# Moving the last unit's k^T v ahead of its scores, into a PSUM bank of an earlier unit

## Chip, cores, metric

The kernel runs on one core of one Trainium2 chip. The metric is device time in microseconds (us) of that core, the median over several executions; lower is better. All timed runs told here are in the fast state, at a granted TensorE clock of 0.999 to 1.000.

## The reference

Causal retention over 8 batches x 8 heads x 576 positions x 64, then a mixture of four experts, all computed for every token. Cut to what matters:

```python
def _attn_ref(q, k, v):                      # (8, 8, 576, 64) each
    scores = scale * q @ k.transpose(0, 1, 3, 2)
    Dmat = where(rel >= 0, gamma ** rel, 0)  # per-head decay, causal
    return (scores * Dmat) @ v

def _moe_ref(x, domain_probs, w1, w2):       # x: (4608, 512)
    p = domain_probs / (domain_probs.sum(-1, keepdims=True) + 1e-9)
    for e in range(4):                       # w1: (4, 512, 1024), w2: (4, 1024, 512)
        out += p[:, e:e+1] * (relu(x @ w1[e]) @ w2[e])
```

## The kernel before

The kernel folds the decay into q and k, so that attention becomes chunks: scores inside a chunk with a 0/1 mask, and a carried state, the running sum of k^T v. Batch 0 is done in four **units**: units 0 and 1 are positions 0 to 255 for heads 0 to 3 and 4 to 7, units 2 and 3 are positions 256 to 511 for the same two groups of heads. Each unit has these steps on TensorE:

- transposes of k and q (`trans_pe`), copied out by ScalarE;
- scores, masked by VectorE into `sT`;
- `kv`: the sums k^T v, copied out of PSUM into `sbd`;
- own values (`values_own`: masked scores times v) and carried values (`values_carried`: q times state), copied out by ScalarE into `xt`, the input of the experts.

PSUM is a ring of four tiles of two banks each. The parts that the change touches:

```python
def kv_open(self, u=0):
    if u == 0:
        self.kvt = ring_tile("kvp0", [128, 2, 2, 2, 128])     # two banks
    self.kvp = self.kvt[:, u]                                 # one of them

def kv_front(self, others=()):                # four matmuls of 256 columns: positions of the first half
    self.kv_mm(128, slice(0, 2), 0, True, others)

def kv(self, fresh=True, others=()):
    hf, kvp = self.hf, None
    front = hf == 1 and self.carry is None
    if fresh:
        self.kv_open()
        if front:
            self.kv_front()
    self.kv_mm(128, 1, hf, not front, others)  # four matmuls of 128 columns
    self.kv_mm(64, 0, hf, False, others)       # four matmuls of 128 columns over 64 rows
    ...                                        # two copies of the sums into sbd:
        self.reads.append(nc.vector.tensor_copy(dst, src) if others else nc.scalar.activation(dst, src, Copy))

for u in range(NU):
    if u + 2 < NU:
        cast_unit(u + 2)
    if u == NU - 1:
        part = UpHalf(0)
        part.matmuls(0)                        # expert 0's first eight products
    us[u].values_own()
    if u + 1 < NU:
        us[u + 1].scores()
    if u == 1:
        us[2].kv(False, us[1].reads)
    us[u].values_carried()
    if u + 2 < NU:
        us[u + 2].trans_pe(1 - u)
    if u in (0, 2):
        us[u + 1].kv()
    if u == 0:
        us[2].kvt = us[1].kvt
        us[2].kv_open(1)                       # unit 2 sums in the second bank of unit 1's tile
        us[2].kv_front(us[1].reads)
part.matmuls(1)
...
```

`others` lists reads of the other bank of the same tile. The matmuls are declared independent of them; without that declaration they would wait, since the tile is tracked as a whole.

Of the kernel before, what the change touches and what calls it, by code (L numbers as in the profile page):

```python
# [11 lines left out]
Copy = mybir.ActivationFunctionType.Copy  # L12
# [11 lines left out]
def kernel(  # L24
# [10 lines left out]
    nc = tc.nc  # L35
# [30 lines left out]
    def ring_tile(name, shape, dt=FP32):  # L66
        return ring.tile(shape, dt, tag="ring", name=name)
# [162 lines left out]
    class Duo:  # L230
# [18 lines left out]
        def kv(self):  # L249
            kvp = ring_tile("kvp", [128, 2, NC, D])  # L250
            for i, p in self.pairs():
                for c in range(NC):
                    for j in range(2):
                        nc.tensor.matmul(kvp[64 * j:64 * j + 64, i, c:NC, :], lhsT=bfs[p % 2]["k"][:, c, j, :],  # L254
                                         rhs=bv[p][:, c, j, :].unsqueeze(1).to_broadcast([128, NC - c, D]),
                                         start=(i == 0 and c == 0), stop=(c == NC - 1), skip_group_check=True)
            for j in range(2):
                r = slice(64 * j, 64 * j + 64)
                nc.scalar.activation(sbd[r, self.ps, :, r], kvp[r], Copy)
# [253 lines left out]
    class Unit:  # L513
# [53 lines left out]
                s[:, :, :, :, :].rearrange("p j g r t -> p (j g) (r t)"),  # L567
                tri0[:, :, :, :].rearrange("p r s t -> p (r s t)").unsqueeze(1).to_broadcast([128, 4, 2 * C]), op=MULT)

        def kv_open(self, u=0):  # L570
            if u == 0:
                self.kvt = ring_tile("kvp0", [128, 2, 2, 2, 128])
            self.kvp = self.kvt[:, u]

        def kv_mm(self, rows, dst, hh, start=False, others=()):
            for g in range(2):
                for r in range(2):
                    two = lambda n: self.bf(n, hh)[0:rows, r, 2 * g:2 * g + 2, :].rearrange("p j d -> p (j d)")
                    rhs = two("v")
                    if dst == slice(0, 2):  # L580
                        rhs = rhs.unsqueeze(1).to_broadcast([rows, 2, 128])
                    mm = nc.tensor.matmul(self.kvp[:, g, dst, :], lhsT=two("k"), rhs=rhs,
                                          start=(start and g == 0 and r == 0), stop=False, skip_group_check=True)
                    for i in others:
                        tc.declare_no_dep(mm.ins, i.ins, reason="another bank of the same tile")
# [4 lines left out]
        def kv(self, fresh=True, others=()):  # L590
            hf, kvp = self.hf, None
            front = hf == 1 and self.carry is None
            if fresh:
                self.kv_open()
                if front:
                    self.kv_front()
            self.kv_mm(128, 1, hf, not front, others)
            self.kv_mm(64, 0, hf, False, others)
            self.reads = []
            kvp = self.kvp  # L600
            gs = slice(2 * self.g, 2 * self.g + 2)
            for j in range(2):
                jr = slice(64 * j, 64 * j + 64)
                dst = sbd[jr, gs, 2 * hf:2 * hf + 2, jr]
                src = kvp[jr, :, :, jr]
                if hf == 1 and self.carry is not None:
                    nc.vector.tensor_tensor(dst, src,
                                            self.carry[jr, gs, :].unsqueeze(2).to_broadcast([64, 2, 2, D]), op=ADD)
                else:
                    self.reads.append(nc.vector.tensor_copy(dst, src) if others else nc.scalar.activation(dst, src, Copy))  # L610
                if hf == 0 and self.carry is not None:
                    nc.vector.tensor_copy(self.carry[jr, gs, :], kvp[jr, :, 1, jr])

# [47 lines left out]
    us = [Unit(0, hf, g, raw0[u], bfv0(g)) for u, (hf, g) in enumerate(units0)]  # L661
# [7 lines left out]
    def cast_unit(u):  # L669
        us[u].cast("k", nc.vector)  # L670
        us[u].cast("q", nc.vector)
        us[u].cast("v", nc.gpsimd)
        for f in load_w1_at.get(u, ()):
            load_w1(0, f)
# [7 lines left out]
# [4 lines that stand above are left out]
            part = UpHalf(0)  # L686
            part.matmuls(0)
        us[u].values_own()
        if u + 1 < NU:
            us[u + 1].scores()  # L690
        if u == 1:
            us[2].kv(False, us[1].reads)
        us[u].values_carried()
        if u + 2 < NU:
            us[u + 2].trans_pe(1 - u)
        if u in (0, 2):
            us[u + 1].kv()
        if u == 0:
            us[2].kvt = us[1].kvt
            us[2].kv_open(1)  # L700
            us[2].kv_front(us[1].reads)
    part.matmuls(1)
    early.close()
    hp = ctx.enter_context(tc.tile_pool(name="hp", bufs=1))
# [190 lines left out]
```

## Time and profile before

| | before |
|---|---|
| device time, median of the first 3 runs | 535.66 us (535.66 to 535.78) |
| span of the profiled run | 534.0 us |
| TensorE busy | 523.8 us, 98% |
| changed stage | about 14.7 to 19.6 us of the span |

In a timeline, a row gives the start, the length, the engine, the line, the instruction with output <- inputs, the number merged into the row, and in brackets the idle time before it with what ended it. Starts are reliable. The ends of matmuls are modelled, so I measure TensorE from start to start. The page and the rows that carry the argument are in the prediction.

### The profile page before, as it was taken

What the parts mean: (1) busy time and instruction counts of PE and PEld (TensorE: products, weight loads), DVE (VectorE), ACT (ScalarE), POOL (GpSimd) and SP (SyncE); (2) the same over time, 40 slices, a digit from 0 to 9 for tenths busy, and PEclk for the clock granted to TensorE, in tenths of its full rate; (3) what the DMA queues carried; (4) which work ended last, traced back from release to release, by engine and by line L of the source; (5) the groups of instructions that cost most, each with busy time, mean ns of one, the idle gap of its engine ahead of it and who ended that gap; (6) DMA issues with size and microseconds to landing.
All of it is one profiled execution on the core that took longest, in us unless ns stands there. A gap on an engine that the chain in (4) does not pass through costs nothing.

```text
span 534.0 us, 10194 instructions
## 1 busy us (share of the span) xinstructions
PE 523.8 (98%) x4220; PEld 341.9 (64%) x4259; DVE 362.3 (68%) x458; ACT 85.3 (16%) x173; POOL 147.3 (28%) x191
## 2 busy tenths in 40 slices
PE   8999999999999999999999999999999999999997
PEld 4644544478745885478646865587548844884486
DVE  5435768895577667697578767776765567557763
ACT  4623440012101121020101001100110000000010
POOL 5744104245245334335132614152000000000000
PEclk9999999999999999999999999999999999999999
DMA  9999947777769967946353655454010111110001
GB/s 239 195 212 243 252 129 193 161 155 163 149 168 161 170 133 150 155 84 163 105 135 96 147 137 113 106 115 129 20 41 22 59 39 41 41 41 20 1 24 56
DMA packets 145054, 63.55 MB, mean 119 GB/s; under 512 B 123760, under 2 KB 135808, under 8 KB 145008
## 3 DMA queue, kind: packets, MB, share of 16 engines
q1 hardware_dynamic: 134080, 43.42, 37.3%
q0 software_dynamic: 10784, 19.35, 16.6%
q8 instruction: 33, 0.54, 0.4%
q10 hardware_dynamic: 144, 0.13, 0.1%
q14 instruction: 13, 0.11, 0.1%
HBM read 53.56 MB, written 9.51 MB: 118 GB/s over the span
## 4 chain that ended last, share of the span: by engine, by line
PE 72%; ACT 2%; DMA 1%; issue 0%; DVE 0%; POOL 0%; POOLq 0%
PE ph L358 35%; PE pd L474 34%; ACT xt L291 2%; PE o L283 1%; DMA qTr<-bfr_q 1%; PE o L278 1%; PE py L474 1%; DVE h L364 0%; PE or L343 0%; PE sr L337 0%; PE or L345 0%; POOL bf_k L238 0%; DVE ob L502 0%; PE kvp L254 0%; POOLq L238 0%
## 5 line engine op out<-in xcount | busy, mean ns | idle before, releaser
L358 PE MATMUL ph<-xt,w 128*128 128x512 bf16 x1102 | 249.0, 379 | 2.5 <-DVE h L364 0.2
L364 DVE SCALAR_TENSOR_TENSOR h<-ph,pB 128x1024 bf16<-128x1024 f32 x128 | 156.4, 1223 | 58.7 <-PE ph L358 58.0
L358 PEld LDWEIGHTS <-w 128*128 128x128 bf16 x1136 | 110.0, 98 | 127.8
L474 PEld LDWEIGHTS <-h 128*128 128x128 bf16 x1024 | 100.0, 98 | 13.3
L474 PEld LDWEIGHTS <-s 128*128 128x128 bf16 x768 | 75.0, 98 | 8.7
L474 PE MATMUL pd<-wx,h 128*128 128x256 bf16 x512 | 61.1, 273 | 0.2
L474 PE MATMUL pd<-wx,s 128*128 128x256 bf16 x512 | 61.1, 273 | 0.0
L219 POOL DMA_DIRECT2D pB<-pd x28 | 15.8, 563 | 153.9 <-DVE h L364 153.2
L509 POOL TENSOR_TENSOR ob<-v,p 128x256 f32<-128x256 f32 x15 | 11.3, 754 | 115.0 <-DVE v L506 93.5
L238 POOL TENSOR_TENSOR bf_k<-raw_k,gk 128x512 bf16<-128x512 f32 x24 | 26.4, 1100 | 36.2 <-DMA raw_k<-in_k_dram 22.6
L270 DVE TENSOR_TENSOR sT<-s,tri 128x1024 bf16<-128x1024 f32 x24 | 28.2, 1219 | 6.4 <-PE s L268 6.4
L291 ACT ACTIVATE xt<-o 128x768 bf16<-128x768 f32 (+6 forms) x24 | 13.0, 594 | 116.8 <-PE o L283 116.8
L474 PE MATMUL pd<-t4w,h 128*128 128x256 bf16 x256 | 30.6, 273 | 0.0
L447 DVE TENSOR_TENSOR s<-s,h 128x1024 bf16<-128x1024 bf16 x32 | 30.2, 985 | 0.0
L397 PE MATMUL po<-wx,h 128*128 128x512 bf16 x124 | 28.6, 379 | 0.3 <-issue 0.2
L474 PE MATMUL pd<-t3w,h 128*128 128x256 bf16 x240 | 28.7, 273 | 0.0
L474 PE MATMUL pd<-t2w,s 128*128 128x256 bf16 x240 | 28.6, 273 | 0.0
L482 ACT ACTIVATE p<-pd 128x256 f32<-128x256 f32 x16 | 6.1, 384 | 138.9 <-PE pd L474 112.8
L238 POOL TENSOR_TENSOR bf_q<-raw_q,gq 128x512 bf16<-128x512 f32 x24 | 26.9, 1123 | 2.3 <-DMA rawr_v<-in_v_dram 1.7
L451 DVE TENSOR_TENSOR s<-h,s 128x1024 bf16<-128x1024 bf16 x32 | 25.6, 838 | 0.0
L445 DVE TENSOR_TENSOR s<-h 128x1024 bf16<-128x1024 bf16 x32 | 24.6, 809 | 0.0
L491 DVE TENSOR_TENSOR u<-pd,p 128x256 f32<-128x256 f32 x15 | 6.4, 425 | 22.7 <-PE pd L474 22.6
(161 smaller groups left out, 375.4 us busy)
## 6 DMA issues: line engine op xcount, KB each, us to landing
pB<-pd POOLq DMA_DIRECT2D x28, 256.0 KB, 3.6
raw_k<-in_k_dram SPq DMA_DIRECT2D x48, 128.0 KB, 2.8
raw_q<-in_q_dram SPq DMA_DIRECT2D x48, 128.0 KB, 3.0
raw_v<-in_v_dram SPq DMA_DIRECT2D x48, 128.0 KB, 3.0
out_dram<-oa SPq DMA_DIRECT2D x16, 256.0 KB, 2.2
out_dram<-ob SPq DMA_DIRECT2D x15, 256.0 KB, 2.0
w<-in_moe_w_dram POOLq DMA_DIRECT2D x3, 1024.0 KB, 14.1
wx<-in_moe_w_dram POOLq DMA_DIRECT2D x3, 1024.0 KB, 15.3
```

What stands on the lines that cost most here:

```text
L219: eng.dma_start(out=pB[t, e], in_=pd[e:e + 1, t * NT:(t + 1) * NT].to_broadcast([128, NT]))
L238: eng.tensor_tensor(bfs[p % 2][n], raw1[n], g[:, :, 2 * p:2 * p + 2].unsqueeze(3).to_broadcast([128, NC, 2, D]), op=MULT)
L270: nc.vector.tensor_tensor(sT[:, :, :, :].rearrange("p j c t -> p (j c) t"), s[:, :, :, :].rearrange("p j c t -> p (j c) t"), tri[:, :].uns ...
L291: nc.scalar.activation(xt_of(t)[:, self.ps, n0 + a - t * NT:n0 + z - t * NT], o[:, :, a:z], Copy)
L358: nc.tensor.matmul(ph[:, f, :], lhsT=w1_sb[e][:, dc, fc * 128:(fc + 1) * 128], rhs=x[:, dc, :], start=(dc == 0), stop=(dc == NDC - 1))
L364: nc.vector.scalar_tensor_tensor(h[:, fk:fk + 2, :], ph, 0.0, pB[t, e][:, :].unsqueeze(1).to_broadcast([128, 2, NT]), op0=MAX, op1=MULT)
L397: nc.tensor.matmul(po[:, gg, :], lhsT=h[:, e * NFC + fc, (2 * m + gg) * 128:(2 * m + gg + 1) * 128], rhs=wx[e // 2][:, (e % 2) * NFC + fc, ...
L445: nc.vector.tensor_tensor(self.alloc("s1")[:, l], h[:, l, self.b], h[:, r, self.b], op=ADD)
L447: nc.vector.tensor_tensor(self.alloc("s2")[:, l], self.s1[:, l], h[:, l, self.a], op=SUB)
L451: nc.vector.tensor_tensor(self.alloc("s4")[:, l], h[:, r, self.a], self.s2[:, l], op=SUB)
L474: mm = nc.tensor.matmul(dst, lhsT=src[:, kk, tok], rhs=rhs(c), start=(start and c == 0), stop=(c == KH - 1), skip_group_check=True)
L509: nc.gpsimd.tensor_tensor(self.ob[:, HF:Dm], self.v, self.p5, op=ADD)
```

## The change

The intent is to fill two holes of TensorE in front of unit 2's values and unit 3's scores with unit 3's k^T v. Its sums go to the bank of unit 1's sums, which have been copied out by then, and the four front matmuls and the other eight get places of their own.

```diff
-        def kv_open(self, u=0):
-            if u == 0:
-                self.kvt = ring_tile("kvp0", [128, 2, 2, 2, 128])
-            self.kvp = self.kvt[:, u]
 ...
             if fresh:
-                self.kv_open()
+                self.kvt = ring_tile("kvp0", [128, 2, 2, 2, 128])
+                self.kvp = self.kvt[:, 0]
 ...
-                    self.reads.append(nc.vector.tensor_copy(dst, src) if others else nc.scalar.activation(dst, src, Copy))
+                    self.reads.append(nc.vector.tensor_copy(dst, src) if not fresh and self.g == 0 else nc.scalar.activation(dst, src, Copy))
 ...
         us[u].values_own()
+        if u == 2:
+            us[3].kv(False, us[2].reads)
         if u + 1 < NU:
             us[u + 1].scores()
 ...
-        if u in (0, 2):
-            us[u + 1].kv()
         if u == 0:
-            us[2].kvt = us[1].kvt
-            us[2].kv_open(1)
+            us[1].kv()
+            us[2].kvp = us[1].kvt[:, 1]
             us[2].kv_front(us[1].reads)
+        if u == 1:
+            us[3].kvp = us[1].kvt[:, 0]
+            us[3].kv_front(us[2].reads)
     part.matmuls(1)
```

## The prediction

> **What bounds the kernel now.** I read the page's busy shares and slices first, then the waits of TensorE, then the timeline of the stage that the diff touches, engine by engine.
>
> ```profile
> PE 523.8 (98%) x4220; PEld 341.9 (64%) x4259; DVE 362.3 (68%) x458; ACT 85.3 (16%) x173; POOL 147.3 (28%) x191
> PE   8999999999999999999999999999999999999997
> PEclk9999999999999999999999999999999999999999
> ```
>
> TensorE is busy in 98% of a 534.0 us span at full clock. Only a stretch in which it idles can give time back. The list of TensorE's waits over the whole span (engine, line, what it waited for: us in total, times, longest) has few entries:
>
> ```profile
> PE w L137 <- DVE zz L130: 1.3, 1, 1.3
> PE s L563 <- ACT qkT L542: 0.8, 2, 0.5
> PE o L625 <- DVE sT L565: 0.5, 1, 0.5
> ```
>
> The first is the start of the program. The other two lie in the first batch's attention, the only code that the diff changes. The TensorE timeline there (start us, us, instruction group, idle before):
>
> ```profile
> 14.74 0.39 PE L540 MATMUL pt<-ident,bf_q 128*128 128x128 bf16 x4
> 15.66 0.42 PE L625 MATMUL o<-sT,bf_v 64*64 64x128 bf16 x16 [0.53 <-DVE sT L565]
> 16.41 0.42 PE L563 MATMUL s<-qkT 64*64 64x128 bf16 x16 [0.33 <-ACT qkT L542]
> 16.76 0.40 PE L635 MATMUL o<-qkT,sbd 128*128 128x128 bf16 x4
> 16.99 1.15 PE L582 MATMUL kvp<-bf_v,bf_k 128*128 128x256 bf16 x12
> 18.07 1.05 PE L379 MATMUL ph<-xt,w 128*128 128x256 bf16 x8
> 19.05 0.42 PE L625 MATMUL o<-sT,bf_v 64*64 64x128 bf16 x16
> 19.40 0.40 PE L635 MATMUL o<-qkT,sbd 128*128 128x128 bf16 x4
> ```
>
> By place in the program these are: the last unit's (unit 3's) transposes of q; unit 2's own values; unit 3's scores; unit 2's carried values; unit 3's k^T v (twelve matmuls: four "front" ones and eight others); expert 0's first eight products; unit 3's own values; its carried values. Two holes are seen: 0.53 us before unit 2's values and, between 15.66 and 16.41, some 0.5 us of start-to-start time beyond the 0.25 us that sixteen such matmuls take elsewhere. From 16.41 on TensorE runs without a hole. What ends the holes is on the other engines:
>
> ```profile
> 14.29 1.22 DVE L565 TENSOR_TENSOR sT<-s,tri 128x1024 bf16<-128x1024 f32 x1
> 15.43 0.84 DVE L610 CAST sbd<-kvp 64x256 bf16<-64x256 f32 x2
> 16.88 1.23 DVE L565 TENSOR_TENSOR sT<-s,tri 128x1024 bf16<-128x1024 f32 x1 [0.61 <-PE s L563]
> 15.33 1.02 ACT L542 ACTIVATE qkT<-pt 128x1024 bf16<-128x1024 bf16 x1
> 17.19 0.77 ACT L651 ACTIVATE xt<-o 128x256 bf16<-128x256 f32 x2 [0.84 <-PE o L635]
> ```
>
> Unit 2's mask multiply on VectorE ends at 15.51, which releases the values at 15.66. The copy of unit 3's transposes on ScalarE ends at 16.35, which releases the scores at 16.41. Unit 3's mask multiply ends at 18.11; it is not waited for, because its values come up only at 19.05.
>
> **What the Trainium skill says.** "TensorE: Matmul & The Clock Gate", "Back-to-back issue gap", gives N/2.4 + 2.5 ns for an isolated matmul and about 81 ns for a sustained stream of N = 128 with a weight load each. The trace has both: 24 products of 256 columns start from 19.64 to 22.26, 109 ns each, and eight k^T v matmuls of 128 columns start from 13.74 to 14.40, 82 ns each. "PSUM — Partial Sum Buffer", "PSUM bank collisions raise a hardware error", asks for two engines to be kept apart by bank and quadrant. That is why the new matmuls may run into the first bank of the shared tile while VectorE copies unit 2's sums out of the second; the kernel before does the same in the other direction at 11.97, with no wait inside the twelve. "Perfetto Trace Analysis", "Identifying the Most-Contended Engine", warns that matmul busy share overstates the nearness to the roofline; I use it here only to find holes, and take costs from start-to-start times.
>
> **The change, part by part.** No matmul, copy or transfer is added or removed. Unit 3's twelve k^T v matmuls move forward from behind unit 2's carried values, split in four and eight; they lose their own PSUM tile and use the first bank of unit 1's. Unit 3's copies out stay on ScalarE and unit 2's on VectorE, since the new condition picks what the old one picked.
>
> Step 1, the front four. Their inputs are unit 1's keys and values, long there, and the bank's old contents are copied out by ScalarE before 14 us. They issue at about 14.96 (the four transposes at 14.74 take 0.22). They have 256 columns: 4 x 0.109 = 0.44, so done issuing by 15.40. This lies wholly inside the hole that ends at 15.66; unit 2's values stay at 15.66.
>
> Step 2, the other eight. They issue behind the sixteen values, at 15.66 + 0.25 = 15.91, and take 0.66 (as at 13.74), so to about 16.57. The hole before the scores ended at 16.41, so 0.5 us of the 0.66 is hidden and the scores start 0.16 later, at about 16.57 instead of 16.41. The copy at 16.35 no longer holds them.
>
> Step 3, what leaves. Behind unit 2's carried values the 1.08 us (16.99 to 18.07) is gone. Scores 0.35 and carried values 0.23 bring TensorE to about 17.15, where expert 0's eight products start; they took 0.98 before (18.07 to 19.05) and would end by 18.05 to 18.13. If nothing else held, unit 3's values would move from 19.05 to 18.13, 0.92 earlier. That is the whole 1.08 less the 0.16.
>
> Step 4, what holds. Unit 3's mask multiply follows its scores by 0.47 (16.41 to 16.88 before), so 16.57 + 0.47 = 17.04, and takes 1.23: it ends at 18.27. From a mask's end to the values was 0.15 (15.51 to 15.66). So the values start at about 18.40, not 18.13: a new wait of about 0.27 us, and a gain of 19.05 - 18.40 = 0.65 us.
>
> Step 5, behind it. Carried values and the rest of expert 0 follow at the same distances: ScalarE has unit 3's state ready at about 17.5 (copies at about 16.7, 0.77 long, now ahead of unit 2's output copy, which goes to about 18.3), before it is read at about 18.75. Everything behind is paced by TensorE, so the 0.65 should reach the end: 535.66 - 0.65 = 535.01.
>
> **The rivals.** A: the full 0.92, or a little more, if the mask is done sooner than I count: 534.7. The uncertainty is in the 0.15 of release and in how the eight matmuls pack behind the values; the VectorE record of 1.23 speaks against it. B: the gain is lost to weights that arrive at an absolute time. TensorE would wait at the first point where it overtakes them. The landing times (us, from issue) are in the views of the DMA issues of short windows:
>
> ```profile
> w<-in_moe_w_dram POOLq DMA_DIRECT2D x1, 1024.0 KB, 14.1
> w<-in_moe_w_dram POOLq DMA_DIRECT2D x1, 512.0 KB, 6.9
> wx<-in_moe_w_dram POOLq DMA_DIRECT2D x2, 512.0 KB, 9.7
> ```
>
> Expert 1's first weights are issued at 17.29, so land at about 31.4; TensorE needed them at 32.62 and will at 31.97. The second half of expert 0's second weights, issued at 15.83, lands at about 26.4 (the two halves average 9.7 and the first has 8.8, so 10.6), needed at about 27.4 before and 26.8 after. The last half of expert 0's first weights, issued at about 13.2, lands at about 20.1 and is needed at 21.6. All have room, but only 0.4 to 0.6 us in the two tightest, and their queue may vary. If one is late by that, the gain falls to 0.2 to 0.5: 535.2 to 535.5. C: the front four wait for unit 2's copies on VectorE (to 16.27) after all, through the shared tile, or a rotated PSUM slot does. Then unit 2's values start at about 16.7, the eight end at 17.6, the mask at 19.3 and unit 3's values start at about 19.45: 0.4 slower, 536.1. Against it: the same exemption worked at 11.97, where twelve matmuls ran through while the other bank waited for its copy. D: later stages, where VectorE is over 90% busy for stretches, fall differently against each other by some tenths; nothing in the trace says in which direction.
>
> **Range and chances.** 535.0 is the sum. The full-gain rival and a lucky later stage give 534.6 as the low end, the late-weights rival 535.5 as the high end. Two per cent is 10.7 us; all holes of TensorE in the changed stage are near 1 us, so even every rival together stays within it. The three runs of before lie within 0.12 us, so the difference should show.
>
> **What would show it right or wrong.** In the changed kernel's TensorE timeline: four 256-column k^T v matmuls between the transposes at 14.74 and the values near 15.66 (step 1); eight of 128 columns behind those values and scores at about 16.6 with no wait for the transposes' copy (step 2); products of expert 0 at about 17.15 (step 3); a new wait of 0.2 to 0.3 us for the mask before unit 3's values at about 18.4 (step 4); the same distance of about 0.65 us at the start of expert 0's down products, 25.71 before, and at the end (step 5). A wait for a weight transfer between 21 and 33 us would be rival B; values of unit 2 starting past 16.2 would be rival C; a shift present at 33 us and absent at the end would be D.

## The result

| | before | changed |
|---|---|---|
| median of 6 runs | 535.61 us (535.24 to 535.78) | 534.88 us (534.69 to 535.04) |
| span of the profiled run | 534.0 us | 533.0 us |

The ratio is 0.9987, with a 95% interval of 0.9975 to 1.0: 0.7 us less by the medians. A ratio is the mean time of one kernel's fast runs over that of the other's of the same rounds, so it is not quite the ratio of the medians quoted beside it.

TensorE's timeline of the changed kernel. The file is four lines shorter at this point: L577 was L582 (k^T v), L621 was L625 (own values), L631 was L635 (carried values), L606 was L610 (copies of the sums), L647 was L651 (copies of the outputs).

```profile
14.89 0.39 PE L540 MATMUL pt<-ident,bf_q 128*128 128x128 bf16 x4
15.11 0.60 PE L577 MATMUL kvp<-bf_v,bf_k 128*128 128x256 bf16 x4
15.68 0.42 PE L621 MATMUL o<-sT,bf_v 64*64 64x128 bf16 x16
16.03 0.72 PE L577 MATMUL kvp<-bf_v,bf_k 128*128 128x128 bf16 x8
16.68 0.42 PE L563 MATMUL s<-qkT 64*64 64x128 bf16 x16
17.04 0.40 PE L631 MATMUL o<-qkT,sbd 128*128 128x128 bf16 x4
17.27 1.04 PE L379 MATMUL ph<-xt,w 128*128 128x256 bf16 x8
18.43 0.42 PE L621 MATMUL o<-sT,bf_v 64*64 64x128 bf16 x16
25.09 1.24 PE L397 MATMUL po<-wx,h 128*128 128x512 bf16 x5
```

The four and the eight stand where they were put, the two bracketed waits of before are gone, and expert 0's products follow the carried values at once. Expert 0's down products start at 25.09 in place of 25.71; the row of before is

```profile
25.71 1.46 PE L397 MATMUL po<-wx,h 128*128 128x512 bf16 x6
```

VectorE's and ScalarE's rows of the same stretch of the changed kernel, and one row of TensorE's weight loads (PEld):

```profile
14.05 1.22 DVE L565 TENSOR_TENSOR sT<-s,tri 128x1024 bf16<-128x1024 f32 x1
17.16 1.23 DVE L565 TENSOR_TENSOR sT<-s,tri 128x1024 bf16<-128x1024 f32 x1 [1.13 <-PE s L563]
14.87 0.77 ACT L647 ACTIVATE xt<-o 128x256 bf16<-128x256 f32 x2 [0.81 <-PE o L631]
16.79 0.77 ACT L606 ACTIVATE sbd<-kvp 64x256 bf16<-64x256 f32 x2 [0.29 <-PE kvp L577]
18.43 0.26 PEld L621 LDWEIGHTS <-bf_v 64*64 64x64 bf16 x16 [0.41 <-DVE sT L565]
```

Unit 3's mask multiply ends at 17.16 + 1.23 = 18.39, and unit 3's values start 0.04 later. The products before them started at 17.27 and take 8 x 0.109 = 0.87, so TensorE started nothing for 18.43 - 18.14 = 0.29 us. Not all of this is a wait for the mask. In the order of before the same eight products take 0.98 up to the values (18.07 to 19.05), with no mask to wait for; here they take 1.16 (17.27 to 18.43), so about 0.18 is the wait. The list of the matmuls' waits doesn't show it: the products' row ends at 17.27 + 1.04 = 18.31 because the end is modelled, which leaves too little idle time to be listed. The list of the weight loads does: unit 3's first one, in the row above, waited for the mask. The Trainium skill explains the end on "Perfetto Trace Analysis", "Tensor Engine Instruction (MATMUL, LD_WEIGHTS)": the reported end is estimated from the instruction's size. The trace agrees: in the profile of before the products' row ends at 18.07 + 1.05 = 19.12, past the start of the values behind them at 19.05.

The first batch's inputs come at slightly different times in each run, and the absolute times of the stage move with them: the transposes of q start between 14.49 and 15.31 in the profiles below. So I compare distances. Three of them add up:

| profile | q transposes to unit 2's values | unit 2's values to first down product | first down product to last product group |
|---|---|---|---|
| before, first profile | 0.92 | 10.05 | 502.91 |
| changed, first profile | 0.79 | 9.41 | 502.54 |

The second column is the stage of the prediction: 0.64 us less. The third is everything behind the stage. It was 0.37 us shorter in this pair of profiles, and with it the spans differ by 1.0, where the medians differ by 0.73. The first profile of before has a wait there, the start of the remainder's scores behind a transposing transfer:

```profile
172.75 0.28 PE L337 MATMUL sr<-qTr,kTr 128*128 128x64 bf16 x4 [0.27 <-DMA qTr<-bfr_q]
```

In the changed kernel these four start at 171.76 with no wait.

### The profile page after: what moved, and what is told of

Read it like the earlier page. It is cut to its first block, busy times and chain, and to the rows that moved or that the text cites. A ratio compares the mean times of both kernels' runs of the same rounds, so it can differ in the third digit from the quotient of the medians.

```text
span 533.0 us, 10194 instructions
## 1 busy us (share of the span) xinstructions
PE 523.9 (98%) x4220; PEld 342.1 (64%) x4259; DVE 361.4 (68%) x458; ACT 85.2 (16%) x173; POOL 147.8 (28%) x191
## 4 chain that ended last, share of the span: by engine, by line
PE 73%; ACT 2%; issue 0%; DVE 0%
PE ph L358 36%; PE pd L474 34%; ACT xt L291 2%; PE o L283 1%; PE o L278 1%; PE py L474 1%; DVE h L364 0%; PE or L343 0%; PE sr L337 0%; PE or L345 0%; DVE ob L502 0%
## 5 line engine op out<-in xcount | busy, mean ns | idle before, releaser
L447 DVE TENSOR_TENSOR s<-s,h 128x1024 bf16<-128x1024 bf16 x32 | 31.5, 1024 | 0.0
L451 DVE TENSOR_TENSOR s<-h,s 128x1024 bf16<-128x1024 bf16 x32 | 24.3, 799 | 0.0
```

Of the source, the lines that this page charges most:

```text
L447: nc.vector.tensor_tensor(self.alloc("s2")[:, l], self.s1[:, l], h[:, l, self.a], op=SUB)
L451: nc.vector.tensor_tensor(self.alloc("s4")[:, l], h[:, r, self.a], self.s2[:, l], op=SUB)
```

## The experiments

Theory: the gain is what leaves TensorE's path between unit 2's values and the down products, limited by unit 3's mask on VectorE, and it goes to the end one for one. Rivals: TensorE's own work alone sets the stage, so that the mask doesn't matter; the place of the sums doesn't matter; or the gain comes from waits behind the stage. Each run was timed in 5 rounds beside the kernel before. The changes are too small for the 2% rule, so every verdict below is "the same" by it; what can be told apart is told from the profiles. The distances from all profiles are in one table at the end of this section.

### 1. The front four alone

```diff
         us[u].values_own()
-        if u == 2:
-            us[3].kv(False, us[2].reads)
         if u + 1 < NU:
             us[u + 1].scores()
 ...
         us[u].values_carried()
 ...
+        if u == 2:
+            us[3].kv(False, us[2].reads)
```

> Only the front four matmuls of unit 3's k^T v move ahead (into the hole before unit 2's values); the other eight stay behind unit 2's carried values, as before. Theory (what leaves the path counts, and the mask of unit 3 is waited for only when scores and products come close behind one another): 0.42 us less than before, so about 535.2; unit 3's values follow expert 0's eight products with no wait for the mask; the hole before the scores is still there. Rival (the move of the eight alone makes the gain, the front hides nothing because unit 2's values are pushed back): as before, 535.6.

Measured: 535.31 us against 535.53, ratio 0.9993 (0.9981 to 1.0005). By time alone it is inconclusive; the profile is not. The second hole is still there, and unit 3's values follow the products with no wait (18.61, against a mask that ends at 16.87 + 1.23 = 18.10):

```profile
16.40 0.42 PE L563 MATMUL s<-qkT 64*64 64x128 bf16 x16 [0.35 <-ACT qkT L542]
```

The stage is 9.64 in place of 10.05: 0.41 us less, the 0.42 that was expected.

### 2. All twelve behind unit 2's values

```diff
-        if u == 1:
-            us[3].kvp = us[1].kvt[:, 0]
-            us[3].kv_front(us[2].reads)
 ...
         if u == 2:
+            us[3].kvp = us[1].kvt[:, 0]
+            us[3].kv_front(us[2].reads)
             us[3].kv(False, us[2].reads)
```

> All twelve k^T v matmuls of unit 3 go behind unit 2's own values and ahead of its scores, none into the first hole. Theory: scores at about 17.0 us, mask ends at about 18.7, unit 3's values at about 18.9, so only 0.15 to 0.25 us less than before: about 535.4, with a longer wait for the mask than in the full change. Rival (TensorE's own work is the bound and the mask is not): the whole hole of 0.5 us is used, 535.1 or less.

Measured: 535.46 us against 535.53, ratio 0.9997 (0.9984 to 1.001). The inputs came late in the profiled run, so the absolute times are all later than expected, but the stage is 9.84: 0.21 us less than before, as expected. The scores come behind all twelve, the mask follows (18.02 to 19.25), and the values start at 19.30, directly behind the mask, so the rival of TensorE as the only bound falls. The wait for the mask was expected to be longer than in the full change, and it is not: the eight products take 1.17 (18.13 to 19.30) up to the values, against 1.16. One row shows a wait that I had not foreseen:

```profile
16.11 0.42 PE L621 MATMUL o<-sT,bf_v 64*64 64x128 bf16 x16 [0.41 <-ACT xt L647]
```

Unit 2's values wait for ScalarE's copy of unit 1's output as well as for their mask.

### 3. Without the exemption from the other bank's copies

```diff
-            us[3].kv_front(us[2].reads)
+            us[3].kv_front()
```

> The full change, but the front four matmuls are not exempted from waiting for unit 2's copies out of the other bank of the tile. Theory: the front starts at about 16.1 to 16.3 us, behind VectorE's copies, everything behind it moves back: unit 3's values at about 19.3, 0.2 to 0.4 us slower than before, 535.8 to 536.0. Rival (the exemption matters little, since the mask of unit 2 comes at nearly the same time): as the full change, 534.9.

Measured: 535.99 us against 535.53, ratio 1.0012 (1.0 to 1.0024); 0.46 us slower by the medians.

```profile
16.53 0.60 PE L577 MATMUL kvp<-bf_v,bf_k 128*128 128x256 bf16 x4 [1.17 <-DVE sbd L606]
17.05 0.42 PE L621 MATMUL o<-sT,bf_v 64*64 64x128 bf16 x16
```

The front waits for VectorE's copies of unit 2 and pushes unit 2's values from 0.79 to 0.91 us behind the transposes to 2.08. The stage behind is 9.41, as in the full change. So the same order without the declaration costs more than the change brings; this was rival C of the prediction, and it is real but avoided.

### 4. A PSUM tile of its own

```diff
-            us[3].kvp = us[1].kvt[:, 0]
-            us[3].kv_front(us[2].reads)
+            us[3].kvt = ring_tile("kvp0", [128, 2, 2, 2, 128])
+            us[3].kvp = us[3].kvt[:, 0]
+            us[3].kv_front()
 ...
-            us[3].kv(False, us[2].reads)
+            us[3].kv(False)
```

> The same order as the full change, but unit 3's k^T v gets a new PSUM tile out of the ring of four in place of unit 1's freed bank. Theory: the next slot of the ring is that of unit 2's scores, so the front waits for unit 2's mask to end (15.3 to 15.5 us) and runs behind it, in place of inside the hole: unit 2's values 0.2 to 0.5 us later than in the full change, time 535.2 to 535.4. Rival (where the sums lie does not matter): as the full change, 534.9.

Measured: 535.54 us against 535.53, ratio 1.0008 (0.9992 to 1.0025), with one of six runs at 538.38; by time no gain is left, where 535.2 to 535.4 was expected. I expected a wait for unit 2's mask; the trace names another:

```profile
15.85 0.60 PE L577 MATMUL kvp<-bf_v,bf_k 128*128 128x256 bf16 x4 [0.41 <-ACT xt L647]
```

The front waits for ScalarE's copy of unit 1's output, so by this row the new tile got the slot of that output, not that of unit 2's scores. (The mask ended at 15.71 and the copy at 15.80, so the times alone wouldn't tell.) The effect is the expected one: the front runs behind the hole, unit 2's values come 1.32 us behind the transposes, and the stage behind is again 9.41. In the distances of the one profile 0.24 us of gain is left. The place of the sums matters: unit 1's bank is free when nothing in the ring is.

### 5. Unit 3's copies on VectorE, ahead of its mask

```diff
-nc.vector.tensor_copy(dst, src) if not fresh and self.g == 0 else nc.scalar.activation(dst, src, Copy)
+nc.vector.tensor_copy(dst, src) if not fresh else nc.scalar.activation(dst, src, Copy)
```

> The full change, but unit 3's two copies out of PSUM run on VectorE, ahead of unit 3's mask, in place of ScalarE. Theory (the mask of unit 3 ends the wait before its values): the mask starts about 0.4 us later (17.5 in place of 17.16), the values at about 18.85 in place of 18.43, time 535.3. Rival (the values were limited by TensorE's own queue): as the full change, 534.9.

Measured: 535.12 us against 535.46; the ratio is 1.0001 (0.9989 to 1.0012), because two of six runs took 536.21 and 536.98, for which I have no profile. The profile of a typical run:

```profile
17.46 1.22 DVE L565 TENSOR_TENSOR sT<-s,tri 128x1024 bf16<-128x1024 f32 x1
18.74 0.42 PE L621 MATMUL o<-sT,bf_v 64*64 64x128 bf16 x16 [0.65 <-DVE sT L565]
```

With the mask held back, the wait grows to where the view lists it, and the values start 0.06 behind the mask's end. The stage is 9.94, 0.53 us more than in the full change. The mask is on the path. The time doesn't show this: four of the six runs took 534.91 to 535.24, about as long as the changed kernel (experiment 8), so the reading rests on the one profile.

### 6. The gain padded away

```diff
     part.matmuls(1)
+    warm(3)          # three 512-column matmuls of zeros
     early.close()
```

> The full change with three idle 512-column matmuls (3 x 0.216 = 0.65 us) behind the first half of expert 0's products, which takes the gain back without a change of order. Theory (everything behind the stage is paced by TensorE, a shift there goes to the end one for one): about 535.5, as before. Rival (the gain at the end comes from waits of later stages, and a shift of the first stage is absorbed): 534.9 to 535.1.

Measured: 535.42 us against 535.46, ratio 1.0 (0.9987 to 1.0012). The rows that bound the stage are

```profile
15.84 0.42 PE L621 MATMUL o<-sT,bf_v 64*64 64x128 bf16 x16
25.89 1.46 PE L397 MATMUL po<-wx,h 128*128 128x512 bf16 x6
```

so it is 10.05, exactly that of before, and the time is that of before too. The changed kernel took 534.78 (experiment 8). A shift of 0.65 us at 20 us reached the end whole; had later waits absorbed such shifts, the time would have stayed near 534.9.

### 7. Twelve products ahead of unit 3's values

If the 0.29 us before unit 3's values is a wait for the mask, more of TensorE's work can stand in it. Four more of expert 0's products go ahead of unit 3's values, and the second half starts with four products whose inputs come from unit 2, which is finished by then, in two different banks, so that they do not run into ScalarE's copies of unit 3.

```diff
             part = UpHalf(0)
-            part.matmuls(0)
+            part.products((0, 1, 2))
 ...
-    part.matmuls(1)
+    part.products((3,))
 ...
     part = UpHalf(1)
-    part.matmuls(0)
-    part.matmuls(1)
+    for dcs in ((0, 1), (2, 3)):
+        part.products((0, 2), dcs)
+    part.products((1, 3))
```

`products(fcs, dcs)` is the loop of `matmuls` over chosen output blocks and input blocks.

> The full change with twelve of expert 0's first sixteen products ahead of unit 3's values in place of eight, and the second half's products in an order that uses unit 3's outputs four matmuls later. Theory (0.25 to 0.3 us of TensorE's time before unit 3's values is a wait for the mask): the wait is filled, unit 3's values at about 18.6, and the start of the down products 0.25 to 0.3 us earlier than in the full change, 534.6. Rival (a wait for unit 3's outputs on ScalarE takes its place in the second half's products): as the full change, 534.9.

Measured: 534.43 us against 535.46, ratio 0.9981 (0.997 to 0.9993).

```profile
17.52 1.47 PE L385 MATMUL ph<-xt,w 128*128 128x256 bf16 x12
18.92 0.42 PE L627 MATMUL o<-sT,bf_v 64*64 64x128 bf16 x16
```

The twelve products take 1.31 (to 18.83), the mask ended at 18.63, and the values follow the products. The stage is 9.24: 0.17 us less than in the full change, where 0.25 to 0.3 was expected. The expectation took the whole 0.29 for a wait; the 0.18 worked out under the result is what there was to gain. No new wait for unit 3's outputs appears.

### 8. The changed kernel again

> The changed kernel once more, on the same chip as the other three, for its time and a second profile. The profile of the first run showed 0.62 us of gain up to 166 us and 0.37 us more from a transposing transfer at 172 us that TensorE did not wait for. Theory (that wait comes and goes from run to run): 534.7 to 535.1, with 0.6 to 0.75 us less than before. Rival (the change moves that wait away for good): about 1.0 us less than before, 534.6 or less.

Measured: 534.78 us against 535.46, ratio 0.9988 (0.9976 to 1.0); 0.68 us less. The stage is 9.41 again. The time is within the range of the theory. Experiment 7 is 0.35 us faster by the medians, which is more than its 0.17 us of profile.

### 9 and 10. Before again, and the twelve products again

> The kernel before, unchanged, for a second profile and as a measure of how far two equal kernels differ here. Theory (the wait of 0.27 us for a transposing transfer at 172 us in the first profile of before is of that run and not of the kernel): no such wait here, 10.05 us from unit 2's values to the first down product as in the first profile, ratio within 0.9993 to 1.0007. Rival (the wait belongs to the kernel before, and the change removes it): the wait is there again, at the same place.

Measured: 535.57 us against 535.57 of before, ratio 0.9999 (0.9986 to 1.0013). The stage is 10.04. The bracketed wait at 172 us is not there, but the remainder's scores start 7.59 us behind the carried values of that place, against 7.85 in the first profile and 7.42 in most profiles of the changed orders: a part of it is.

> The version with twelve products ahead of unit 3's values once more, next to the kernel before. From the profiles: 9.24 us from unit 2's values to the first down product, against 9.41 in the full change and 10.05 before, so 0.8 us less than before at the end: 534.6 to 534.8. Rival (the 1.0 us of the first timing is the real one, so something behind the stage gains as well): 534.4 or less.

Measured: 534.88 us against 535.57, ratio 0.9988 (0.9975 to 1.0). Four of the five runs took 534.62 to 534.91; the profiled run took 535.55, and its profile shows why:

```profile
16.26 0.61 POOL L533 CAST bf_v<-raw_3v 128x512 bf16<-128x512 f32 x1 [2.15 <-DMA raw_3v<-in_v_dram]
16.93 0.71 PE L583 MATMUL kvp<-bf_v,bf_k 128*128 128x128 bf16 x8 [0.84 <-POOL bf_v L533]
```

In this run unit 3's values arrived late. Their cast ended at 16.87 in place of about 15.1, and the eight matmuls, which now stand more than a microsecond earlier, waited for it. In the order of before the twelve started at 16.99 in the first profile, so by these times the same lateness would have been hidden. The extra gain of experiment 7 over the full change did not come back in time: 0.69 us less than before here, where the full change had 0.73 and 0.68.

### 11 and 12. The late cast on purpose

The same three transfer issues put ahead of the cast of unit 3's values on GpSimd, in both kernels:

```diff
+        if u == 3:
+            load_w2(0, 0, NFC // 2)
+            load_w2(0, NFC // 2, NFC)
+            nc.gpsimd.dma_start(out=p0, ...)
         us[u].cast("v", nc.gpsimd)
 ...
-    load_w2(0, 0, NFC // 2)
-    load_w2(0, NFC // 2, NFC)
-    nc.gpsimd.dma_start(out=p0, ...)
     load_w1(1)
```

> The kernel before, but GpSimd issues the next three transfers ahead of its cast of unit 3's values, so that the cast ends at about 16.9 us in place of 15.1. Theory (in the order of before, unit 3's k^T v reads these values only past 17 us): no cost, 535.4 to 535.7. Rival (the earlier weight transfers or the shifted queue change the time by themselves): more than 0.3 us away from before.

> The same late cast in the changed kernel. Theory (the change reads unit 3's values about one microsecond earlier and so lives on the slack of that cast): the eight matmuls wait from about 16.0 to 16.9 us, unit 3's values at about 19.3, and the gain is gone: 535.5 to 535.8. Rival (some other slack covers it): as the full change, 534.9.

Measured: 535.28 us (ratio 1.0001, 0.9988 to 1.0015) for the order of before and 535.34 us (ratio 1.0002, 0.999 to 1.0015) for the changed order, against 535.38. Both times lie below their expected ranges (535.4 to 535.7 and 535.5 to 535.8), and both are as long as before: the gain of the changed order is gone, in all five runs (535.16 to 536.19). But the profile doesn't let me claim the expected cause. In the changed order:

```profile
15.60 0.66 POOL L527 CAST bf_v<-raw_3v 128x512 bf16<-128x512 f32 x1
16.31 0.71 PE L577 MATMUL kvp<-bf_v,bf_k 128*128 128x128 bf16 x8
```

The cast ended at 16.26, earlier than planned, and delayed the eight by only some 0.06 us; the stage is 9.47. What kept the time up in this run lies elsewhere. Behind the stage it took 502.88 us in place of 502.47, with a listed wait of 0.2 us for the same transposing transfer as in the first profile of before. And the stage began late, with the transposes of q at 15.11 against 14.49 in the profile of the order of before: the first unit's q arrived late in this run, and its transposes waited 0.52 us for it at 5.79. One profile can't say what took the gain in the other four runs. So the pair is inconclusive as a measure of the cast's slack, and why the gain is gone stays open; it settles another point: that later wait also comes in the changed order.

### All distances

From the start of the q transposes to unit 2's values, from there to the first down product, and from there to the start of the last group of products, in us, one profile each:

| kernel | to unit 2's values | stage | behind |
|---|---|---|---|
| before; again; late cast | 0.92; 0.92; 0.91 | 10.05; 10.04; 10.05 | 502.91; 502.64; 502.76 |
| changed; again; late cast | 0.79; 0.91; 0.78 | 9.41; 9.41; 9.47 | 502.54; 502.47; 502.88 |
| 1 front four alone | 0.89 | 9.64 | 502.47 |
| 2 twelve behind | 0.80 | 9.84 | 502.47 |
| 3 no exemption | 2.08 | 9.41 | 502.48 |
| 4 own tile | 1.32 | 9.41 | 502.48 |
| 5 copies on VectorE | 0.79 | 9.94 | 502.48 |
| 6 padded | 0.89 | 10.05 | 502.48 |
| 7 twelve products; again | 0.89; 0.79 | 9.24; 10.14 (late cast) | 502.47; 502.70 |

## Why the prediction was right

- **Step 1 held, with one more party in it.** The front four lie in the hole. Unit 2's values stay at 15.66 (15.68 in the first profile, 15.80 in the second, where the mask came later). In the first profile it was not the mask that set them but ScalarE's copy of unit 1's output, which ended at 15.64 with the mask long done at 15.27. I had not listed that wait. In the other profiles of the changed orders it and the mask end within 0.15 us of each other, except in the changed order with the late cast, where it ends 0.39 later (15.84 against 15.45). It costs next to nothing: in experiments 3 and 4 the front four take 0.52 and 0.53 up to the values, so TensorE itself wasn't ready before about 15.11 + 0.53 = 15.64.
- **Step 2 was a little short.** The eight came 0.35 behind the values and not 0.25, and the scores at 16.68 and not 16.57. The 0.25 was read from values followed by scores, both of 64x64 shape; here a 128-row shape follows. On "TensorEngine Tiling (Array Packing)", "Key Properties", the Trainium skill says that a change of tiling mode drains the array. The trace of before agrees in the direction: sixteen matmuls of own values take 0.25 when scores of the same shape follow (13.17 to 13.42) and 0.35 when carried values of the full shape follow (19.05 to 19.40). That the drain makes the difference was not tested.
- **Step 3 held.** Products at 17.27 where 17.15 was expected; the 0.11 of step 2 is in it.
- **Step 4 held in its mechanism; its sum came out right by luck, from two errors that cancel.** The mask ended at 18.39 (expected 18.27), and the values followed in 0.04 (expected 0.15). They start at 18.43 (expected 18.40). With the expected 0.15 the gain would have been 0.11 smaller. The new wait is about 0.18, not 0.27: the prediction counted 0.98 for the eight products up to the values, and on that count TensorE was free at 17.27 + 0.98 = 18.25. Experiments 2, 5 and 7 show that it is the mask: held back, it holds the values back; with more work in front, the wait is gone. The distances say it once more: in all seven profiles in which only scores, carried values and eight products stand before the values and the copies are where they were (the three of the changed kernel, experiments 2, 3, 4 and 6), unit 3's values start 1.75 us after unit 3's scores, while TensorE's own work there is 0.35 + 0.23 + 0.98 = 1.56.
- **Step 5 held.** The stage is 0.64 us shorter (0.65 predicted) in both plain profiles of the changed kernel, and experiment 6 shows that such a shift goes to the end. The medians moved by 0.73 and 0.68 us. The predicted time was 535.0; measured are 534.88 and 534.78.
- **The rivals.** A (0.92) fell by the mask. B, in the form I wrote it, was not seen: no profile lists a wait of TensorE between 21 and 33 us. A relative of B that I missed was: unit 3's own values, in one profile, cost the gain of that run. C is real (experiment 3, 0.46 us slower than before) and is what the exemption avoids. D exists as a few tenths behind the stage. The wait at 172 us stood as the fourth entry of the list from which the prediction shows three (`PE sr L337 <- DMA qTr<-bfr_q: 0.3, 1, 0.3`); it wasn't taken up.

**What stays open.** Everything behind the stage takes 502.47 or 502.48 us in eight of the fourteen profiles and 0.07 to 0.44 more in the other six. In four of these (all three of the order of before, and the changed one with the late cast) the whole excess lies between the carried values at about 165 us and the remainder's scores at about 172, where the transposing transfer is waited for: 7.85, 7.59, 7.70 and 7.83 us in place of 7.42. Only two of the four list the wait, but the transfer itself was slower in all four: it landed 5.4 to 5.7 us after its issue, and 4.3 to 5.0 in the eight profiles without excess. So the order of before meets this wait in three profiles of three, the changed orders clearly in one of eleven. Whether it belongs to the order of before or to the phase of a run is not decided: the padded kernel has the stage of before and not this wait. The medians differ by only 0.04 and 0.09 us beyond 0.64, which is less than the 0.17 to 0.44 of the three profiles of before and within their scatter. What took the gain in experiment 12 is open too. The two slow runs of experiment 5 and the one of experiment 4 have no profile.

## What to carry to other kernels

Work moved into a hole ahead of a dependent chain (here k^T v ahead of scores, mask, values) pushes that chain back by whatever doesn't fit, so the gain is found by following the chain to its next meeting with the busy engine and not by adding up the holes. When a moved instruction shares a buffer, check what it is made to wait for: the same order gained 0.64 us in a bank declared independent, at most 0.24 us in a tile of its own (by one profile; by time nothing) and lost 0.46 us without the declaration. Moving work earlier also spends slack of its inputs, which shows only in the runs where an input comes late.

## What the Trainium skill lacked or had wrong

- "TensorEngine Tiling (Array Packing)" says that a mode change drains the array but gives no figure. Here a change from 64x64 to 128-row shapes goes with 0.10 us more (0.25 against 0.35 from start to start of sixteen matmuls of own values).
- I found on no page how long a TensorE instruction takes to start after the end of the VectorE or ScalarE instruction that it waits for. Here unit 3's values start 0.04 to 0.06 us after the mask in the changed order, and unit 2's 0.14 to 0.15 after theirs where the mask, and not ScalarE's copy, came last. In the changed kernel's traces a semaphore instruction of 51 ns stands ahead of unit 2's values (at 15.3 and 15.7 us in the two plain profiles) and none ahead of unit 3's; that this makes the 0.1 us was not tested.
- "Perfetto Trace Analysis" says that matmul ends are estimated, but not that a real wait can vanish from a list of the matmuls' waits by it: about 0.18 us did here, and the weight loads' list showed it (as 0.41).
